# Transposes of the second chunk on VectorE; clamp and integer addition of the weight conversion on GpSimd

## Chip, cores and metric

One core of one Trainium2 chip. The metric is the device time of one execution in microseconds (us), as the median of several executions. An experiment is given with the kernel before, run on the same chip in the same rounds. All runs compared here are of the fast state; one execution of the kernel before, of 1321.95 us, is marked slow in the record and left out of the ratios. A ratio is the mean time of one kernel's fast runs over the mean of the other's of the same rounds, so it is not quite the ratio of the medians that stand beside it.

## The reference

```python
# batch 4, heads 8, sequence 768, head size 48; d_model 384, d_ff 1536; weights arrive as float64
f = 1 / (1 + exp(-f_logit))
for t in range(S):                        # HGRN2: a state per head, decayed by f
    state = f[:, :, t, :, None] * state + einsum('bhd,bhe->bhde', k[:, :, t], v[:, :, t])
    y[:, :, t] = einsum('bhd,bhde->bhe', q[:, :, t], state)
x = y.transpose(0, 2, 1, 3).reshape(B * S, H * D)
out = (silu(x @ w_gate) * (x @ w_val)) @ w_out
```

## The kernel before

The sequence is cut into six chunks of 128 steps. A chunk and one of the four batches make a "unit": units 0 to 3 are the first chunk, 4 to 7 the second. While the products of one chunk run on TensorE, the attention units of the next are worked in between. During the first chunk's products the weights are also brought from float64 words to float32, in 18 pieces of 128x768.

q, k and f have to be transposed. In the first `SQUARES` chunks TensorE does that, from double-buffered raw tiles; in later chunks VectorE does it from 32x32 squares, and then both buffers together are one "room":

```python
SQUARES = 2
...
if c >= SQUARES:
    nc.scalar.activation(squares("f"), squares("f"), AF.Sigmoid)
    nc.vector.transpose(in_turn(pairs(gate)[:, :, 1:N1]), squares("f"))          # L494
else:
    p = transposed("fTp", fr)                                                    # TensorE, L488
    nc.scalar.activation(pairs(gate)[:, :, 1:N1], p, AF.Sigmoid)
...   # L502: scan for the tails
if c >= SQUARES:
    nc.vector.transpose(in_turn(kT), squares("k"))                               # L514
    nc.vector.transpose(in_turn(qT), squares("q"))                               # L515
    load_after(u)
else:
    kp, qp = transposed("kTp", kr), transposed("qTp", qr)                        # TensorE, L488
nc.vector.tensor_tensor(kT, kp, pairs(tail, 2)[:, :, 0:C], ALU.mult)             # L520
nc.vector.tensor_tensor_scan(head, gate[:, 0:n], start, 1.0, ...)                # L522
nc.vector.tensor_tensor(qT, qp, pairs(head)[:, :, 1:N1], ALU.mult)               # L523
...   # TensorE: scores sc (L535), kT transposed (L542), y (L561, L565), dS (L589)
```

A piece of the weights passes three engines. SyncE fetches the words (three buffers), ScalarE takes out two parts (two buffers each), and VectorE joins them in four steps (code abridged):

```python
def fetch():  nc.sync.dma_start(out=w64, in_=src)                                 # L423
def sizes():  up  = nc.scalar.activation(lo, Copy, scale=2.0 ** -29)              # L432
              top = nc.scalar.activation(hi, Abs)                                 # L434
def join():
    nc.vector.tensor_scalar(top, top, MIN, MAX, op0=ALU.max, op1=ALU.min)         # L440 clamp
    nc.vector.tensor_scalar(top, top, 3, 0x3FFFFFFF, shift_left, bitwise_and)     # L442 shift
    nc.vector.scalar_tensor_tensor(top, hi, -(1 << 30), top, and, or)             # L443 merge
    nc.vector.tensor_tensor(dst.bitcast(I32), top, up, ALU.add)                   # L444 addition
```

A scheduler orders the instructions of each engine, by its own estimates. In the traces an engine takes them in that order: one that waits holds up those behind it (2.90 us in run e7, below).

## Time and profile before

| | before |
|---|---|
| median (range) of 3 executions | 642.0 us (641.66 to 642.87) |
| TensorE (PE) busy of the 641.2 us span | 632.4 us, 99% |
| VectorE (DVE), ScalarE (ACT), GpSimd (POOL) | 73%, 29%, 3% |
| mean granted TensorE clock | 0.999 |

TensorE is full (it waits 3.7 us in all for others), so the table is read through TensorE.

### The profile page before, as it was taken

To read this page: it belongs to the slowest core of one execution; us is meant where nothing else is said; L and a number is where in the kernel's file an instruction comes from. 1 tells how busy PE (TensorE), PEld (TensorE's weight loads), DVE (VectorE), ACT (ScalarE), POOL (GpSimd) and SP (SyncE) were. 2 spreads that over 40 slices of the span, in tenths; PEclk is the share of its full clock that TensorE was granted. 3 is DMA by queue.
4 is the path that set the end of the run, shared out by engine and by line. 5 is a ranking of instruction groups with operands and counts; after the bars stand their busy time and mean duration, and the time that the engine had idled before them with its cause. 6 is when DMAs were issued, how large, how long until landed. Compare 5 with 4: busy or idle time off the path is not lost.

```text
span 641.2 us, 10398 instructions
## 1 busy us (share of the span) xinstructions
PE 632.4 (99%) x4014; PEld 522.3 (81%) x4014; DVE 471.0 (73%) x802; ACT 186.6 (29%) x284; POOL 22.4 (3%) x39
## 2 busy tenths in 40 slices
PE   8999999999999999999999999999999999999996
PEld 5954555667888899888999888899888889988896
DVE  6889779988987875896966787877497862366631
ACT  1566366204632212523221614130321210021100
POOL 1000000000000010010000010000000000000000
PEclk9999999999999999999999999999999999999999
DMA  9987456333230324130324321132411001100001
GB/s 193 234 212 225 127 141 206 102 81 101 67 92 6 94 67 132 50 75 26 75 52 131 91 49 50 32 80 65 123 38 49 15 24 23 54 0 1 0 1 54
DMA packets 98393, 51.89 MB, mean 81 GB/s; under 512 B 56864, under 2 KB 92192, under 8 KB 98336
## 3 DMA queue, kind: packets, MB, share of 16 engines
q1 hardware_dynamic: 95024, 46.63, 28.7%
q10 hardware_dynamic: 3312, 4.52, 2.0%
q8 instruction: 33, 0.54, 0.4%
q14 instruction: 24, 0.20, 0.1%
HBM read 42.47 MB, written 4.72 MB: 74 GB/s over the span
## 4 chain that ended last, share of the span: by engine, by line
PE 98%; DMA 1%; DVE 0%; SPq 0%; issue 0%
PE p L760 32%; PE o L824 19%; PE c L760 13%; PE o L671 5%; PE val L647 5%; PE gate L647 5%; PE sc L535 4%; PE y L565 3%; PE o L877 3%; PE y L561 2%; PE kt L542 2%; PE dS L589 2%; PE y L582 1%; DMA fraw<-in_f_logit_dram 1%; PE idle L356 1%; PE fTp L488 1%
## 5 line engine op out<-in xcount | busy, mean ns | idle before, releaser
L703 DVE TENSOR_TENSOR rest<-u,p 128x512 f32<-128x512 f32 x90 | 61.2, 685 | 43.8 <-PE p L760 43.4
L760 PE MATMUL p<-xT,w_val 128*128 128x256 f32 x240 | 71.4, 379 | 0.0
L760 PE MATMUL p<-xT,w_gate 128*128 128x256 f32 x240 | 71.4, 379 | 0.0
L703 DVE TENSOR_TENSOR u<-u,p 128x512 f32<-128x512 f32 x90 | 61.9, 687 | 10.4 <-PE p L760 8.5
L824 PE MATMUL o<-w_out,h 128*128 128x192 f32 x360 | 62.0, 329 | 0.0
L790 ACT ACTIVATE h<-rest 128x768 f32<-128x768 f32 x30 | 25.3, 844 | 123.6 <-DVE rest L703 123.6
L824 PEld LDWEIGHTS o<-w_out,h 128*128 128x128 f32 x360 | 58.2, 190 | 1.7 <-ACT u L842 1.1
L760 PE MATMUL c<-xT,w_gate 128*128 128x256 f32 x180 | 54.9, 387 | 0.0
L760 PE MATMUL c<-xT,w_val 128*128 128x256 f32 x180 | 53.5, 379 | 0.0
L760 PEld LDWEIGHTS p<-xT,w_val 128*128 128x128 f32 x240 | 45.6, 190 | 6.2
L760 PEld LDWEIGHTS p<-xT,w_gate 128*128 128x128 f32 x240 | 45.6, 190 | 6.2
L537 DVE TENSOR_TENSOR A<-sc,causal 128x512 f32<-128x512 f32 x48 | 31.5, 685 | 10.4 <-PE sc L535 10.4
L760 PEld LDWEIGHTS c<-xT,w_val 128*128 128x128 f32 x180 | 34.2, 190 | 4.6
L527 POOL TENSOR_TENSOR decayed<-state,tails 128x192 f32<-128x192 f32 x20 | 19.7, 986 | 504.3 <-DVE state L593 360.2
L760 PEld LDWEIGHTS c<-xT,w_gate 128*128 128x128 f32 x180 | 32.5, 190 | 5.2 <-issue 0.9
L760 PE MATMUL p<-xs,sv 128*128 128x256 f32 x120 | 35.7, 379 | 0.0
L760 PE MATMUL p<-xs,sg 128*128 128x256 f32 x120 | 35.7, 379 | 0.0
L791 DVE TENSOR_TENSOR h<-h,rest 128x768 f32<-128x768 f32 x30 | 28.8, 962 | 9.1 <-ACT h L790 9.1
L768 ACT COPY u<-c 128x512 f32<-128x512 f32 x30 | 17.4, 581 | 53.8 <-PE c L760 32.1
L647 PE MATMUL val<-xT,w_val 128*128 128x512 f32 x72 | 32.3, 594 | 0.0
L647 PE MATMUL gate<-xT,w_gate 128*128 128x512 f32 x72 | 32.3, 594 | 0.0
L502 DVE TENSOR_TENSOR_SCAN tails<-gates,ones 128x516 f32<-128x516 f32 x24 | 29.4, 1224 | 3.9 <-POOL decayed L527 2.1
(127 smaller groups left out, 1076.6 us busy)
## 6 DMA issues: line engine op xcount, KB each, us to landing
fraw<-in_f_logit_dram SPq DMA_DIRECT2D x64, 96.0 KB, 3.0
kraw<-in_k_dram SPq DMA_DIRECT2D x64, 96.0 KB, 2.2
qraw<-in_q_dram SPq DMA_DIRECT2D x64, 96.0 KB, 2.2
v<-in_v_dram SPq DMA_DIRECT2D x24, 192.0 KB, 3.5
w<-in_moe_w_gate_dram SPq DMA_DIRECT2D x6, 768.0 KB, 4.6
w<-in_moe_w_val_dram SPq DMA_DIRECT2D x6, 768.0 KB, 5.1
w<-in_moe_w_out_dram SPq DMA_DIRECT2D x6, 768.0 KB, 5.6
out_dram<-ob ACTq DMA_DIRECT2D x23, 192.0 KB, 2.5
```

What stands on the lines that cost most here:

```text
L502: nc.vector.tensor_tensor_scan(tail[:, 0:n][:, ::-1], gate[:, 0:n][:, ::-1], ones[:, ::-1], 1.0, op0=ALU.mult, op1=ALU.add)
L527: nc.gpsimd.tensor_tensor(decayed[:, :, 0:D], states[b], whole.broadcast_to((128, HP, D)), ALU.mult)
L535: nc.tensor.matmul(sc[par][:, a * C:(a + 1) * C], lhsT=kT[r, a, :], rhs=qT[r, a, :], start=True, stop=True)
L537: nc.vector.tensor_tensor(A[:, par], sc[par].rearrange("p (a t) -> p a t", t=C), causal.unsqueeze(1).broadcast_to((128, HP, C)), ALU.mult)
L565: nc.tensor.matmul(place(a, par), lhsT=v_[:, 2 * a + par, :], rhs=A[:, par, a, :], start=False, stop=a >= HP - 2, skip_group_check=True)
L647: nc.tensor.matmul(p, lhsT=w[:, i, j * 128:(j + 1) * 128], rhs=xT[c][:, i, :], start=(i == 0), stop=(i == KT - 1))
L671: nc.tensor.matmul(p, lhsT=h[n // 2][:, n % 2 * 2 + b // 2, b % 2 * C:(b % 2 + 1) * C], rhs=w_out[:, j, :], start=(n == 0), stop=(n == NF ...
L703: nc.vector.tensor_tensor(dst, a, b, ALU.add)
L760: nc.tensor.matmul(p[:, n, :], lhsT=lhsT, rhs=rhs, start=first and n == 0, stop=last, skip_group_check=True)
L790: nc.scalar.activation(h[j][:, 1:4, :], rest[:, :, 0, :], AF.Silu)
L791: nc.vector.tensor_tensor(h[j][:, 1:4, :], h[j][:, 1:4, :], rest[:, :, 1, :], ALU.mult)
L824: nc.tensor.matmul(p[:, n, :], lhsT=lhsTs[j][:, n * C:(n + 1) * C], rhs=rhs[:, j, :], start=first and j == 0 and n == 0, stop=last and j = ...
```

## The change

The intent: VectorE takes the transposes of units 4 to 7 from TensorE, and GpSimd, which is 3% busy, takes two of VectorE's four steps of every piece so that VectorE has room.

```diff
-    SQUARES = 2
+    SQUARES = 1
...
-            nc.vector.tensor_scalar(top.bitcast(FP32), top.bitcast(FP32), as_float(0x38000000), as_float(0x47F00000),
+            nc.gpsimd.tensor_scalar(top.bitcast(FP32), top.bitcast(FP32), as_float(0x38000000), as_float(0x47F00000),
                                     op0=ALU.max, op1=ALU.min)
...
-            nc.vector.tensor_tensor(dst.bitcast(I32), top, up, ALU.add)
+            nc.gpsimd.tensor_tensor(dst.bitcast(I32), top, up, ALU.add)
```

## The prediction

> **What bounds the kernel now.** I read the page's busy table first, then TensorE's own waits, then busy time by stretch, then the order of time around single instructions, and last the groups by form.
>
> ```profile
> PE 632.4 (99%) x4014; PEld 522.3 (81%) x4014; DVE 471.0 (73%) x802; ACT 186.6 (29%) x284; POOL 22.4 (3%) x39
> ...
> PE idle L356 <- DVE ones L348: 2.1, 1, 2.1
> PE fTp L488 <- DMA fraw<-in_f_logit_dram: 0.8, 1, 0.8
> PE o L877 <- DVE ob L703: 0.4, 1, 0.4
> PE y L565 <- DVE A L537: 0.2, 1, 0.2
> PE y L582 <- DVE A L537: 0.2, 1, 0.2
> ```
>
> TensorE (PE) is busy 632.4 of 641.2 us and waits 3.7 us in all. So work taken off PE is worth its full time, and any new wait of PE costs its full time. The changed part is the stretch in which the first chunk's products run while the second chunk's four attention units (numbered 4 to 7) and the 18 weight pieces are prepared beside them:
>
> ```profile
> 36.00:66.00 30.00, 30.00 (x133) 14.73 (x132) 28.80 (x45) 19.59 (x25) 1.17 (x1) 1.00 0.76 217
> ...
> 112.00:149.00 37.00, 37.00 (x194) 23.19 (x189) 34.33 (x46) 6.02 (x12) 1.61 (x2) 1.00 0.34 90
> ```
>
> Columns: length, then busy time of PE, weight loads, DVE (VectorE), ACT, POOL (GpSimd). PE is full, DVE is at 96% and 93%: DVE has no room for transposes unless something leaves it. This is why the two parts of the change come together.
>
> **What the change removes from PE.** Three groups of four transposes in each of four units:
>
> ```profile
> 71.07 0.60 PE L488 MATMUL kTp<-idf,kraw 128*128 128x128 f32 x4
> 71.50 0.60 PE L488 MATMUL qTp<-idf,qraw 128*128 128x128 f32 x4
> 71.94 5.32 PE L647 MATMUL gate<-xT,w_gate 128*128 128x512 f32 x12
> ```
>
> From start to start a group takes 0.435 us (its 0.60 overlaps what follows). 12 x 0.435 = 5.2 us. At the first unit less is won: its three groups (34.46 to 35.77) fill time in which PE would wait anyway, as the last copy to xT ends at 35.14 on ACT. The first gate product can start at about 35.3, not 34.5. So 4.3 us are won.
>
> **What it moves between DVE and GpSimd.** The rows by form (busy, mean ns):
>
> ```profile
> L440 DVE TENSOR_SCALAR top<-top 128x768 f32<-128x768 f32 x18 | 10.0, 553 | 10.6 <-ACT top L434 10.6
> L444 DVE CUSTOM_DVE_ANT_0 w_gate<-top,up 128x1536 uint16<-128x1536 uint16 x6 | 5.7, 953 | 0.8 <-PE gate L647 0.8
> L515 DVE STREAM_TRANSPOSE qT<-qraw 128x512 f32<-128x512 f32 x16 | 18.6, 1160 | 0.2 <-PE y L561 0.2
> L514 DVE STREAM_TRANSPOSE kT<-kraw 128x512 f32<-128x512 f32 x16 | 17.9, 1118 | 0.0
> L494 DVE STREAM_TRANSPOSE gates<-fraw 128x512 f32<-128x512 f32 x16 | 17.4, 1088 | 0.0
> ```
>
> DVE loses 18 x (0.553 + 0.95) = 27 us and gains 4 x (1.09 + 1.12 + 1.16) = 13.5 us: 13.5 us lighter. GpSimd has no such instruction yet; I estimate from its 128x192 multiply, which takes 0.515 us where nothing disturbs it. A fill of 128 columns takes 0.205 us and one of 64 takes 0.157, so some 0.1 us is fixed: (0.515 - 0.1) / 192 = 2.1 ns per column. The integer addition (768 columns) is then 0.1 + 1.65 = 1.75 us. The clamp has one input: I take 1.0 us, between 0.75 and 1.3. In all 18 x 2.75 = 50 us of GpSimd's 114, which is not a bound by itself.
>
> [...]
>
> ```profile
> 41.80 0.94 DVE L443 SCALAR_TENSOR_TENSOR top<-w,top 128x768 int32<-128x768 int32 x1
> 41.97 1.17 POOL L527 TENSOR_TENSOR decayed<-state,tails 128x192 f32<-128x192 f32 x1 [38.68 <-DVE tails L502]
> 42.65 0.52 DVE L505 TENSOR_TENSOR least<-least,tails 128x4 f32<-128x4 f32 x1
> ```
>
> The multiply of 0.52 us takes 1.17, ending 0.4 after L443 ends (42.74); then the tiny L505, else 0.17, ends with it. [...]
>
> **The order of the changed program decides it.** I compared the order of instructions on each engine, as built. A piece used to go ACT, then four DVE instructions. Now it goes ACT (1.65 us), GpSimd clamp, DVE shift and merge (0.6 + 0.9), GpSimd addition: two hand-overs more, in three in-order queues, with only two buffers. On PE the units are no longer split: scores, kT transposes, y and dS stand together (about 2.6 us after the scores end), and the next product waits for GpSimd. With durations from the trace and about 0.1 us per hand-over I walked PE's queue:
>
> 1. First val product. ACT ends its piece at 36.75 as before. Then the clamp[...]; a transpose stands between shift and merge on DVE, and GpSimd clamps the next piece first; the addition ends at 42.2 (no contention) to 44.2. PE wants it at 40.45. Wait 1.8 to 3.9, say 3.0.
> 2. Scores of unit 5. Its q transpose needs qT, which y of unit 4 has just been reading; 1.06 + 0.69 against 1.47 us of PE work: 0.5.
> 3. Third val pair, after unit 5. From the end of the scores: kt copy, ACT's next piece (to 3.0), its clamp (4.05), and only then, in GpSimd's order, the addition that PE needs (5.8). PE is there at 2.6: 3.3.
> 4. Scores of unit 6. They follow a val product at once, while DVE's order is: multiply of that product, q transpose, q times head. 0.1 + 0.6 + 1.15 + 0.7 + 0.06 = 2.6, whatever GpSimd does.
> 5. Fifth gate pair, after unit 6: as 3, 3.2.
> 6. Scores of unit 7: as 4, 2.6.
> 7. First down product: mask multiply 1.3, shift and merge 1.5, addition 1.75, against 2.6: 2.1.
> 8. Last third of the down products, after unit 8, which the new order draws forward: as 3, 3.25.
> 9. First product of the next chunk. DVE begins the weight sums about 6 us after the scores of unit 8 and needs 13 us until the token sums; PE wants them at 17.3: 1.5.
>
> Sum 22.0 us. All else waits for nothing that is not there. Net: 22.0 - 4.3 = +17.7, thus 660 us. I take 657, as such a walk leaves some waits too long and the clamp may be quicker.
>
> **The rivals.** *The plain gain:* DVE had no room before and has 13.5 us more now, so the new transposes hide and PE keeps its 4.3 to 5.2 us: 637 to 638. For it: 100% busy PE, a lighter DVE, fewer and larger packets for the loads. Against it: waits 4 and 6, which already cost 5.2 us and need no assumption on GpSimd. *A wash:* GpSimd is quick[...], only waits 1, 4, 6, 7 and half of the rest remain: some 14 - 4.3 = +10, 652. [...] *Loads late:* with one raw buffer for q, k and f, loads of a unit wait for the transposes of the one before. Landing takes 3 us and a unit's turn 20; no bound, I think.
>
> **Range and chances.** 647 to 666 runs from half of the waits to all of them with contention. Faster by 2% would need under 629.2, more than PE's removed work: 0.02. Slower by 2% starts at 654.8; my sum lies above it and the wash below: 0.63. Within: 0.35.
>
> **What would show it.** Right: PE busy near 627 us; PE waits on the additions (line 444 on GpSimd) of about 12 to 16 us in some six places; two waits of 2.6 us of scores on the q multiply (line 523); DVE busy about 457; additions at 1.75 us or more, clamps about 1.0. Wrong: PE still full from 36 to 149 (then the walk misread the order or the queues), or additions far under 1.75 us, or DVE waits for loads, or waits of PE that lie after this stretch.

Three of its figures, held against the pages. The clamp's 1.0 us is the author's estimate, since the trace before has no clamp on GpSimd; it lies between some 0.7 us, an estimate for 768 columns from the two fills (0.157 us for 64, 0.205 for 128), and the 1.75 of the addition. Hand-overs in that trace took 0.03 us (36.75 to 36.78, ScalarE to VectorE) and 0.08 (41.89 to 41.97, VectorE to GpSimd). Packets: 98393 of 527 bytes in the mean before, 92826 of 585 after, over all DMA.

## The result and the profile after

The changed kernel takes 685.27 us (681.87 to 685.55, 4 executions) beside 641.87 us before on the same chip: a ratio of 1.066 (95% interval 1.0625 to 1.0696). The results are correct. The prediction had the direction, but 685 lies far outside of 647 to 666.

The page's busy table and the row of the granted clock, kernel after:

```profile
PE 643.5 (94%) x3966; PEld 525.6 (77%) x3966; DVE 473.0 (69%) x778; ACT 189.3 (28%) x286; POOL 104.3 (15%) x75
...
PEclk9989996989899999999999999999999999999999
```

Two things are seen. TensorE stands idle 683.5 - 643.5 = 40.0 us instead of 8.8. And it is busy 643.5 us although 12 x 0.435 = 5.2 us of transposes have left it: 627.2 were due, so 16.3 us more went into the same work. The clock row says where: of the first eleven slices, one has a 6 and three have an 8; before, the mean clock was 0.999. The trace also keeps each change of the granted clock, of which the views show only means: in the changed kernel it is half in six stretches between 42.9 and 182.9 us, one of 3.41 and five of 6.83 us, 37.5 us together; they start 11, 6, 3, 8 and 11 times 3.41 us apart. In the kernel before it is full from 11.5 to 639.6 us.

TensorE's waits, kernel after (columns: what waited, what released it, us in total, times, longest):

```profile
PE val L647 <- POOL w_val L444: 9.1, 2, 5.0
PE sc L535 <- DVE qT L523: 7.0, 4, 3.7
PE o L671 <- POOL w_out L444: 6.4, 2, 4.7
PE gate L647 <- POOL w_gate L444: 3.6, 1, 3.6
```

In the order of time around instructions (start, duration, in brackets the idle time before), kernel after:

```profile
44.07 8.22 PE L647 MATMUL val<-xT,w_val 128*128 128x512 f32 x12 [4.12 <-POOL w_val L444]
52.13 5.31 PE L647 MATMUL gate<-xT,w_gate 128*128 128x512 f32 x12
...
72.01 1.16 PE L535 MATMUL sc<-qT,kT 48*128 48x128 f32 x16 [0.52 <-DVE qT L523]
...
101.83 2.08 PE L535 MATMUL sc<-qT,kT 48*128 48x128 f32 x16 [3.67 <-DVE qT L523]
```

A pair of products takes 5.31 us, but 8.22 right after a wait of 4.12. Scores take 1.16 us, but 2.08 after a wait of 3.67. So these two waits are paid twice: as idle time, and as a slow stretch after it.

Busy time by stretch, kernel after, for the two stretches shown before (columns as there):

```profile
36.00:66.00 30.00, 25.88 (x71) 11.69 (x70) 18.76 (x25) 12.41 (x16) 18.51 (x8) 0.89 0.48 128
112.00:149.00 37.00, 34.43 (x128) 18.25 (x129) 18.51 (x26) 15.39 (x22) 20.07 (x10) 0.83 0.47 129
```

Now no engine is full. VectorE fell from 28.80 to 18.76 us of 30, GpSimd stands at 18.51, TensorE at 25.88: everybody waits for somebody.

The groups by form, kernel after (busy, mean ns | idle before, by releaser):

```profile
L440 POOL TENSOR_SCALAR top<-top 128x768 f32<-128x768 f32 x18 | 51.3, 2854 | 44.0 <-ACT top L434 44.0
L444 POOL TENSOR_TENSOR w_gate<-top,up 128x768 int32<-128x768 int32 x6 | 10.9, 1812 | 8.7 <-DVE top L443 8.7
L442 DVE TENSOR_SCALAR top<-top 128x768 int32<-128x768 int32 x18 | 17.6, 977 | 25.3 <-POOL top L440 25.3
```

The addition takes 1.81 us, as estimated (1.75). The clamp takes 2.77 us where nothing disturbs it (mean 2.85), not 1.0. VectorE's shift has grown from 0.56 to 0.98 us in the mean. Twelve of the 18 still take 0.56; four, which start just after an addition, take 2.15, and two, which start just after a clamp, 1.17. A clamp, an addition and a shift:

```profile
107.34 2.77 POOL L440 TENSOR_SCALAR top<-top 128x768 f32<-128x768 f32 x1 [7.61 <-ACT top L434]
110.07 1.80 POOL L444 TENSOR_TENSOR w_gate<-top,up 128x768 int32<-128x768 int32 x1
110.14 2.15 DVE L442 TENSOR_SCALAR top<-top 128x768 int32<-128x768 int32 x1 [1.37 <-POOL top L440]
```

The shift ends 0.42 us after the addition does (112.29 and 111.87), and the other three 0.41 after theirs. The multiply of unit 4 in the prediction looks the same: 1.17 us for 0.52 beside VectorE's merge, ending 0.4 after it. The two shifts beside a clamp end before it does (148.98 and 150.51 in one case), so the clamp did not hold them up for the whole of its length.

### The profile page after: what moved, and what is told of

The parts are those of the page before. It is cut to its first block, busy times and chain, and to the rows that moved or that the text cites. A ratio compares the mean times of both kernels' runs of the same rounds, so it can differ in the third digit from the quotient of the medians.

```text
span 683.5 us, 10365 instructions
## 1 busy us (share of the span) xinstructions
PE 643.5 (94%) x3966; PEld 525.6 (77%) x3966; DVE 473.0 (69%) x778; ACT 189.3 (28%) x286; POOL 104.3 (15%) x75
## 2 busy tenths in 40 slices
DMA packets 92826, 54.26 MB, mean 79 GB/s; under 512 B 45152, under 2 KB 86624, under 8 KB 92768
## 4 chain that ended last, share of the span: by engine, by line
PE 83%; DMA 4%; DVE 4%; SPq 3%; POOL 2%; issue 2%; ACT 1%; ACTq 0%; DVEq 0%; POOLq 0%
PE p L760 29%; PE o L824 18%; PE c L760 11%; PE val L647 4%; PE gate L647 4%; PE sc L535 4%; PE o L877 3%; PE y L565 2%; PE y L561 2%; PE o L671 2%; DMA fraw<-in_f_logit_dram 2%; PE kt L542 1%; POOL top L440 1%; DMA xT<-yT 1%; SPq L576 1%
## 5 line engine op out<-in xcount | busy, mean ns | idle before, releaser
L527 POOL TENSOR_TENSOR decayed<-state,tails 128x192 f32<-128x192 f32 x20 | 17.8, 891 | 389.4 <-DVE state L593 284.8
L440 POOL TENSOR_SCALAR top<-top 128x768 f32<-128x768 f32 x18 | 51.3, 2854 | 44.0 <-ACT top L434 44.0
L647 PE MATMUL val<-xT,w_val 128*128 128x512 f32 x72 | 36.3, 659 | 9.1 <-POOL w_val L444 9.1
L671 PE MATMUL o<-w_out,h 128*128 128x384 f32 x96 | 34.7, 524 | 6.4 <-POOL w_out L444 6.4
L647 PE MATMUL gate<-xT,w_gate 128*128 128x512 f32 x72 | 35.1, 640 | 4.2 <-POOL w_gate L444 3.6
L535 PEld LDWEIGHTS sc<-qT,kT 48*128 48x128 f32 x384 | 25.0, 198 | 15.6 <-DVE qT L523 8.5
L647 PEld LDWEIGHTS val<-xT,w_val 128*128 128x128 f32 x72 | 15.1, 214 | 28.4 <-issue 18.3
```

The source lines that it names most:

```text
L440: nc.gpsimd.tensor_scalar(top.bitcast(FP32), top.bitcast(FP32), as_float(0x38000000), as_float(0x47F00000), op0=ALU.max, op1=ALU.min)
L527: nc.gpsimd.tensor_tensor(decayed[:, :, 0:D], states[b], whole.broadcast_to((128, HP, D)), ALU.mult)
L535: nc.tensor.matmul(sc[par][:, a * C:(a + 1) * C], lhsT=kT[r, a, :], rhs=qT[r, a, :], start=True, stop=True)
L647: nc.tensor.matmul(p, lhsT=w[:, i, j * 128:(j + 1) * 128], rhs=xT[c][:, i, :], start=(i == 0), stop=(i == KT - 1))
L671: nc.tensor.matmul(p, lhsT=h[n // 2][:, n % 2 * 2 + b // 2, b % 2 * C:(b % 2 + 1) * C], rhs=w_out[:, j, :], start=(n == 0), stop=(n == NF ...
```

## The experiments

Eighteen kernels ran, three rounds each and five for the last two. Medians in us; "before" on the same chip had medians of 641.9 to 643.05.

| run | what | median (range) | ratio (95% interval) |
|---|---|---|---|
| e1 | transposes alone | 667.72 (663.86–673.34) | 1.037 (1.032–1.042) |
| e2 | GpSimd alone | 685.55 (685.33–685.87) | 1.067 (1.064–1.070) |
| e3 | transposes, addition moved | 670.50 (668.49–671.36) | 1.044 (1.041–1.047) |
| e4 | transposes, clamp moved | 677.68 (675.75–678.85) | 1.054 (1.051–1.057) |
| e5 | whole change, TensorE kept busy in waits | 678.56 (677.28–682.08) | 1.058 (1.053–1.062) |
| e6 | whole change, clamp of one operation | 679.16 (677.66–681.68) | 1.057 (1.053–1.060) |
| e7 | transposes alone, units split | 664.91 (663.62–665.98) | 1.035 (1.032–1.038) |
| e8 | whole change, units split | 676.17 (675.69–676.83) | 1.053 (1.050–1.056) |
| e9 | e7 with two qT | 673.98 (671.27–675.06) | 1.046 (1.041–1.051) |
| e10 | e9, VectorE in stated order | 673.17 (670.92–673.42) | 1.045 (1.041–1.050) |
| e11 | e10, addition moved | 675.92 (672.84–680.16) | 1.053 (1.046–1.060) |
| e12 | whole change as e10, three buffers | 688.83 (684.92–691.68) | 1.072 (1.066–1.078) |
| e13 | whole change, a third of the clamp | 670.76 (665.71–671.74) | 1.041 (1.036–1.047) |
| e14 | e13, TensorE kept busy in waits | 666.35 (665.23–669.44) | 1.038 (1.033–1.042) |
| e15 | e7 without a clamp | 665.75 (664.53–669.29) | 1.038 (1.034–1.042) |
| e16 | before without a clamp | 644.35 (642.47–646.40) | 1.004 (1.000–1.008) |
| e17 | transposes alone, order of before | 669.38 (667.92–671.96) | 1.041 (1.038–1.045) |
| e18 | e17, fetches ahead of loads | 654.17 (653.41–657.28) | 1.019 (1.016–1.022) |

All gave correct results.

### The change in its parts (e1 to e4)

e1 is the diff's first line alone, e2 its other two, e3 and e4 the first with one of the other two.

> Second chunk's units with VectorE transposes, clamp and addition left on VectorE. Theory A (the long GpSimd clamp, 2.77 us, makes the waits, and each wait over some 2.5 us also halves the clock for 3 us after it): most of the loss goes; two waits of about 2.6 us for the scores that follow a val product at once stay, with slow clock behind them, and VectorE, 13.5 us heavier, adds some: 648 to 658 us. Theory B (the order with whole units standing together is the cause, wherever the clamp runs): 670 us or more, waits of 20 us or more.

> Clamp and addition on GpSimd, the second chunk's units with TensorE transposes as before; TensorE's order is the one of before, with split units. Theory A: the chain to the first val product still is some 4 us late and its clock drop costs 3 more; later pieces have several us of slack: 648 to 660 us. Theory B: at most 3 us over before, 642 to 645 us.

> As the change, but the clamp stays on VectorE; only the addition (1.8 us) goes to GpSimd. Theory A: near e1, 646 to 658 us, since the 2.77 us clamp is out of the chain. Theory B: the order is that of the change, so 670 us or more.

> As the change, but the addition stays on VectorE; only the clamp (2.77 us) goes to GpSimd. Theory A: worse than e3 by 5 us or more, 660 to 678 us. Theory B: the same as e3 within 4 us.

Both parts lose on their own (3.7% and 6.7%), and together they lose no more than the worse one (6.6%). So neither theory holds as it stood: the loss is not GpSimd's alone, nor the transposes' alone. With the transposes, moving both steps costs 685 - 668 = 17 us; the clamp moved alone costs 10 (e4) and the addition alone 3 (e3), the latter within the range of e1's own executions.

e2 shows what the way over GpSimd costs with no transposes moved. The shift's row and the scores of one unit, run e2:

```profile
L442 DVE TENSOR_SCALAR top<-top 128x768 int32<-128x768 int32 x18 | 20.4, 1134 | 42.8 <-POOL top L440 42.8
```

```profile
101.00 2.08 PE L535 MATMUL sc<-qT,kT 48*128 48x128 f32 x16 [8.90 <-DVE qT L523]
```

VectorE stands 42.8 us in front of shifts whose clamp is not done. Its queue is in order, so the q multiply of a unit (L523), which needs nothing from GpSimd, stands behind the shift, and TensorE waits 8.90 us for it. GpSimd was busy 25.16 of the 30 us from 66 to 96 there.

### Half clock and clamp size, in the whole change (e5, e6, e13, e14)

In these four the order of the instructions on TensorE, VectorE, ScalarE and GpSimd was held to that of the changed kernel, so that only the named thing differs (in e13 two neighbours in VectorE's queue swapped). Lines are shifted in them: L710 and L702 are products, L549 and L542 scores. The edits are abridged.

```diff
 # e5: matmuls without a reader, into the bank that the group itself overwrites
+    fill(p, {("val", 0): 12, ("val", 4): 15, ("gate", 8): 9}.get((name, j), 0))
+    fill(sc[0], {2: 9, 3: 6}.get(b, 0))            # second chunk, units 6 and 7
 # e6: the clamp's lower bound alone
-    nc.gpsimd.tensor_scalar(top, top, MIN, MAX, op0=ALU.max, op1=ALU.min)
+    nc.gpsimd.tensor_scalar(top, top, MIN, None, op0=ALU.max)
 # e13: the clamp on 256 of 768 columns (right for these weights only, which reach no bound)
+    part = top[:, 0:1, 0:256]
+    nc.gpsimd.tensor_scalar(part, part, MIN, MAX, op0=ALU.max, op1=ALU.min)
 # e14: e13 and fills of 6, 8, 7, 5 and 5
```

> The changed kernel with the order of its instructions on TensorE, VectorE, ScalarE and GpSimd held to what it was, and 51 idle bf16 matmuls of 128x512 put ahead of five of the six groups that wait longest: first val pair (12), third val pair (15), scores of unit 6 (9), fifth gate pair (9), scores of unit 7 (6). They write the bank that the group itself overwrites, so the results stay right. The last third of the down products, which waits 4.71 us, gets none and serves as a control within the run. Theory C (a wait of TensorE of more than about 2 us makes it run at half rate for the next 3 to 6 us): the groups after the five waits take 5.31 (pairs) and 1.16 us (scores) again and not 8.22, 6.80, 8.43, 2.08 and 2.00; the down products after their wait stay slow; 2.9 + 1.5 + 2.4 + 3.1 + 2.0 = some 12 us less, 671 to 675 us, mean clock 0.985 or more. Rival D (the groups are slow because of what GpSimd and VectorE do to the operands or the memory at that time): the groups stay at 8.2 and 2.0 us, and the time at 683 to 688.

Around two of the filled groups, run e5:

```profile
39.53 2.75 PE L361 MATMUL val<-ones 128*128 128x512 bf16 x12
45.36 7.11 PE L710 MATMUL val<-xT,w_val 128*128 128x512 f32 x12 [3.08 <-POOL w_val L449]
...
96.78 2.10 PE L361 MATMUL sc<-ones 128*128 128x512 bf16 x9
100.64 1.16 PE L549 MATMUL sc<-qT,kT 48*128 48x128 f32 x16 [1.75 <-DVE qT L534]
```

Four of the five filled groups ran at full speed again; the first, where the fill left 3.08 us of idle time, did not, and neither did the last third of the down products, the control. (Behind the scores of unit 7, full speed themselves, y was slow all the same.) The time at half clock fell from 37.5 to 13.7 us. The operands and the work of the other engines were the same, so the slow groups are slow because TensorE stood idle before them, which is theory C. Of the 12 us expected only 6.7 came back (685.27 to 678.56): TensorE reached the later groups earlier, and GpSimd's pieces did not come earlier, so part of the gain turned into waits.

> The changed kernel, all orders held, with the clamp on GpSimd reduced to its lower bound (one operation, not two; these weights never reach the upper bound, so the results stay right). Theory E (the clamp is long because GpSimd pays for each of the two operations): the clamp takes 1.4 to 1.6 us instead of 2.8, each just-in-time chain of a piece is 1.2 us shorter, TensorE's waits on pieces shrink by some 7 to 10 us and the clock recovers part of its loss: 666 to 676 us. Rival F (its cost is per element read and written, whatever the operations): the clamp stays at 2.6 to 2.9 us and the time at 683 to 688.

```profile
L440 POOL TENSOR_SCALAR top<-top 128x768 f32<-128x768 f32 x18 | 40.0, 2225 | 50.0 <-ACT top L434 49.9
```

That is the clamp's row of e6. Neither E nor F: one operation takes 2.13 us undisturbed, two take 2.77. A clamp 0.63 us shorter gained 6 us.

> The changed kernel, all orders held, with the clamp on GpSimd applied to 256 of the 768 columns only (no weight of this input reaches a bound, so the results stay right; the kernel would be wrong for others). It should take 0.9 to 1.1 us, the length that the prediction took for the whole clamp. Theory K (the missing terms are the clamp's size and the half clock): the one-operation run lost 6 us for 0.63 us less of clamp, so 1.8 us less give some 17 us: 664 to 671 us, the two waits of scores at 2.6, the waits on pieces near the predicted 3.0, 3.3, 3.2, 2.1, 3.25, and groups after waits over 2 us at half rate still. Rival L (something else bounds the pieces, buffers or ScalarE): 676 to 686 us.

> The run before, and idle bf16 matmuls (5 to 8 each, 31 in all) ahead of the same five groups as in the filled run, fewer as the waits are shorter. Theory K: no half clock in those groups, 6 to 10 us less than the run before, 655 to 663 us, which is the prediction's 657 to 660 plus nothing else. Rival L: 670 or more.

The clamp's row of e13:

```profile
L441 POOL TENSOR_SCALAR top<-top 128x256 f32<-128x256 f32 x18 | 21.4, 1187 | 56.1 <-ACT top L434 56.0
```

It takes 1.06 us undisturbed, which is the 1.0 that the prediction took for the whole. The time falls by 14.5 us to 670.8 (expected 664 to 671). Now the walk of the prediction can be held against a trace with its own clamp. The nine waits measured in e13 are 1.2, 0.5, 3.0, 3.7, 1.5, 2.6, 0, 3.5 and 1.4, together 17.4 us; the walk had 3.0, 0.5, 3.3, 2.6, 3.2, 2.6, 2.1, 3.25 and 1.5, together 22.0. TensorE was busy 640.9 us where 627.2 were due: 13.7 us are half clock, which the walk lacked. e14 took 4.4 us of this back and ended at 666.4, above the 655 to 663 expected; it still had slow groups after the shorter fills, one slow gate pair before all fills (7.04 us for 5.31, after a wait of only 0.66), and one wait of 4.2 us at the next chunk's first products, which the profile puts down to no releaser. That rest stays open.

### TensorE's order (e7, e8)

The changed order puts a unit's scores, y and dS together. These two hold TensorE to the order in which the program states it. It is that of the kernel before, with the transposes left out, except that unit 8 still stands ahead of the last down products, as in the changed kernel.

```diff
+        since = traced[-1]
         take_turns(pieces, attention_steps(c + 1) if c + 1 < NCH else [], 2 if c else 8)
+        if c == 0:
+            in_order(since, (mybir.EngineType.PE,))
```

> The transposes alone (clamp and addition on VectorE), with TensorE's order in the first chunk's stretch held to the order in which the program states it, which is the order of the kernel before with the transposes left out: units split, scores apart from y and dS. Theory G (what costs 3.7% in the transposes alone is the clustered order): 636 to 648 us, TensorE waits under 12 us in all. Theory B (VectorE has no room for 13.5 us more): VectorE's queue is late all the same, waits of 20 us or more, 660 to 672 us.

> The whole change, with TensorE's order held to the same stated order (units split). If the clustered order is what exposes the GpSimd chain, the waits of the scores of units 6 and 7 (3.67 and 2.57 us) and those of the products right after a unit fall away: 655 to 668 us. If GpSimd's chain of some 6 us per piece bounds the stretch whatever the order, as in the run with GpSimd alone, the time stays at 680 to 690 us.

The order is worth 9 us in the whole change and some 3 in the transposes alone (the ranges overlap): a part, not the cause. e7 fell in rival B's range, e8 between its two. In e7 a unit's waits moved to the pieces:

```profile
66.52 1.16 DVE L515 STREAM_TRANSPOSE qT<-qraw 128x512 f32<-128x512 f32 x1 [2.90 <-PE y L561]
```

VectorE's copy of q stood 2.90 us at the head of its queue until the unit before had read the single qT. The weight piece behind it came late and TensorE waited 4.04 us for it.

### Looking for the cost of the transposes alone (e9 to e12, e15, e16)

```diff
 # e9: two buffers for qT.  e10: VectorE held to the stated order as well.
-        qT = att.tile([128, HP, C], FP32, tag="qT", name="qT")
+        qT = att.tile([128, HP, C], FP32, tag="qT", name="qT", bufs=2)
 # e11: e10 with the addition on GpSimd.  e12: the whole change as e10, and three buffers for up and top, four for w64.
 # e15: e7 without the clamp.  e16: the kernel before without the clamp (both right for these weights only)
```

> The run with the transposes alone and split units, with two buffers for qT. In that run VectorE's q transpose stood 2.90 us at the head of its queue until y of the unit before had read qT, with a finished-but-for-VectorE weight piece behind it, and TensorE then waited 4.04 us for that piece. Theory H (the write of the transposed q straight into the single qT is what costs): VectorE no longer waits for y (3.7 us in the stretch, two times), the waits of 4.0 and 4.3 us lose 3 us or more each and the half clock after them, 648 to 658 us. Rival I (the order of VectorE's queue, units ahead of pieces, costs on its own): the piece behind the unit is late as before, 660 to 666 us.

> As the run before, and VectorE's order of the stretch is also held to the order in which the program states it, in which a piece is finished before the work of the next unit starts. Theory I: pieces come in time, the waits on them fall under 8 us together, 634 to 645 us. If VectorE simply has no room for 13.5 us more: it is busy 28 of 30 us in each stretch and the time stays at 650 or more.

> As the run before, with the integer addition on GpSimd (1.8 us a piece, 33 us in all) and the clamp left on VectorE. VectorE is 17 us lighter and never waits on GpSimd within a piece, as the addition is its last step. If the addition is harmless where the order is good: at or up to 5 us under the run before. If its 0.85 us more of latency a piece[...] still cost: 5 to 15 us above it.

> The whole change, with everything given to it that the runs so far ask for: TensorE's and VectorE's stated order, two qT, and three buffers for each step of a piece in place of two (four in place of three for the fetched words). If buffers and orders were what cost, 640 to 655 us. If a piece's way over GpSimd (clamp 2.8, addition 1.8, with VectorE standing still between them) bounds the stretch in itself, 665 us or more, with VectorE waiting 30 us or more for the clamp.

> The run with the transposes alone and split units, one qT, with the clamp left out altogether (results stay right for this input, not in general): VectorE 10 us lighter, nothing on GpSimd. Theory B (VectorE's load is what makes the transposes lose): most of the loss of 23 us against the kernel before goes, 642 to 650 us. If the longer chain of a unit (two copies that stand in VectorE's queue ahead of the scores) is the cause whatever the load: 655 to 664 us.

> The kernel before with the clamp left out (right for this input only), as a control: VectorE 10 us lighter in a stretch where TensorE is already 100% busy. All theories: 639 to 643 us, the same within 0.5%. Should it be faster by over 1%, then TensorE was not the bound of that stretch.

No run here bore out the theory that it was built for. Two rivals came nearer: e12 met its own (over 665, and VectorE over 30 us before its clamps), and e10 took over 650 us, but with VectorE busy 22 to 27 of 30 us, not 28. e9 took VectorE's wait for y away and was 9 us slower than e7: the scheduler, free to place the copy, put other work in the way. e10's order brought the pieces of gate and val in time (2.6 us of waits) but the scores (8.1) and the pieces of the down products (9.9) late. e11 gained nothing from a VectorE that was 11 us less busy (476.6 for 487.5). In e12 more buffers did not help the chain over GpSimd: VectorE still stood 33.1 us before its clamps. e15 took 10 us from VectorE and stayed at e7's time within the ranges, which speaks against VectorE's load as what then bound it; the control e16 moved by no more than 0.4%.

The trace of e15 gave the next theory. A piece's ScalarE step waited 8.46 us for its words, and SyncE, which issues fetches, loads and stores in order, had issued nothing from 48 to 64 us: it stood for the stores of unit 4's y, with the next fetch behind them.

### SyncE's queue (e17, e18)

e17 is the transposes alone with the order of the kernel before on TensorE, VectorE, ScalarE, and for SyncE's fetches and stores; each VectorE transpose stands directly before the instruction that uses it. The loads of f, k and q stay free. e18 differs in SyncE's order alone: fetches stand ahead of the loads that have to wait.

```diff
 # SyncE's order around unit 5's loads: F a fetch of weight words
-   F(gate) f5 k5 q5 v5 F(val) F(gate) F(val)          # e17
+   F(gate) f5 F(val) F(gate) k5 q5 v5 F(val) F(gate) F(val)   # e18
```

> The transposes alone (nothing on GpSimd), with the order of TensorE, VectorE and ScalarE in the first two chunks' stretches, and of SyncE's weight fetches and stores to xT, held to that of the kernel before: TensorE's without the transposes, VectorE's with each transpose directly ahead of the instruction that uses it; the loads of q, k and f are free. Theory M (the order of the queues that the change brings is what costs, above all fetches behind stores): 636 to 645 us, no wait of SyncE over 8 us on a store ahead of fetches in the stretch, TensorE waits of 12 us or less. If the longer chain of a unit through VectorE costs by itself: 650 us or more, with the waits of TensorE on VectorE's scores or pieces as before.

> The run before (transposes alone, orders of the kernel before), and SyncE's order also fixed for the stretch: a weight fetch stands ahead of each load of f, k and q that has to wait for a copy by VectorE, in the order of the times at which the kernel before issued its fetches. All other engines' orders are the same as in the run before. Theory N (fetches held behind loads that wait for the single room are what costs): no wait of ScalarE over 5 us for a weight's words, no wait of VectorE over 4 us on ScalarE, 15 us or more less than the run before, 640 to 654 us. Rival B (VectorE has 118 us of work in 120 us and everything just in time waits for it): 660 to 670 us, VectorE busy 28 of 30 us from 36 to 66.

SyncE's queue, run e17 and then e18 (start, us in the queue):

```profile
45.75 1.74 SPq L403 DMA_DIRECT2D kraw<-in_k_dram  x4
51.99 1.73 SPq L403 DMA_DIRECT2D qraw<-in_q_dram  x4
53.77 1.69 SPq L408 DMA_DIRECT2D v<-in_v_dram  x1
55.51 0.58 SPq L423 DMA_DIRECT2D w<-in_moe_w_val_dram  x1
```

```profile
42.68 0.39 SPq L423 DMA_DIRECT2D w<-in_moe_w_val_dram  x1
49.43 0.39 SPq L423 DMA_DIRECT2D w<-in_moe_w_gate_dram  x1
49.87 1.91 SPq L403 DMA_DIRECT2D kraw<-in_k_dram  x4
51.87 2.62 SPq L403 DMA_DIRECT2D qraw<-in_q_dram  x4
```

In e17 the load of unit 5's q goes out at 51.99, right after VectorE's copy of unit 4's q (50.89 to 51.97), because the two share one room. The val fetch behind it goes out at 55.51 and not at 42.68. What that does further down, on ScalarE and VectorE, run e17:

```profile
61.65 0.90 ACT L432 ACTIVATE up<-w 128x768 int32<-128x768 uint32 x1 [13.75 <-DMA w<-in_moe_w_val_dram]
```

```profile
63.37 0.56 DVE L440 TENSOR_SCALAR top<-top 128x768 f32<-128x768 f32 x1 [8.61 <-ACT top L434]
```

e17 missed theory M's 636 to 645. With SyncE's order changed and nothing else, the time falls from 669.4 to 654.2 us, at the edge of theory N's range. What is left in e18, first TensorE's waits, then busy time from 36 to 66, then the longest wait:

```profile
PE sc L535 <- DVE qT L523: 8.1, 3, 3.5
...
PE o L671 <- DVE h L663: 2.0, 1, 2.0
```

```profile
36.00:66.00 30.00, 27.00 (x106) 12.68 (x106) 29.52 (x45) 17.40 (x23) 1.06 (x1) 1.00 0.73 214
```

```profile
105.28 1.25 PE L535 MATMUL sc<-qT,kT 48*128 48x128 f32 x16 [3.49 <-DVE qT L523]
```

TensorE no longer waits long for a weight piece (0.5 us). It waits 8.1 us for the q multiply, in three waits. One of them (3.00 us, at 52.70) falls where VectorE is busy 29.52 of 30 us, as rival B has it: no room for the copies. The others (1.60 at 78.91 and 3.49 at 105.28) fall where it is busy 23.87 and 26.92 of 30, and shortly before them VectorE had itself stood 2.11 and 1.81 us for ScalarE. So rival B can hold for a part of the rest at most, and no run took work off VectorE in e18 to test it. TensorE's busy time is 630.2 us, and the 12 us by which e18 is above the kernel before are waits. No version here beats the kernel before.

## Why the prediction was wrong

Against the walk's 660 the changed kernel is 25 us too slow. In its trace TensorE is idle 31.2 us more than before, where the walk had 22.0, and busy 11.1 us more, where the walk had 4.3 less. So two steps failed, the cost of the clamp and the speed after a wait, and the second is the larger in the trace.

**Right: direction, places, addition.** The kernel is slower, and the waits lie where the walk put them: all but the seventh and ninth were found on the named instruction and releaser. The second and sixth had the predicted length (0.52 and 2.57 us); the seventh, first down product, was 0, with 1.69 us one piece later; the ninth was 1.84 us but behind ScalarE's output copy, not the weight sums. The addition was right to 0.06 us.

**Wrong: "The clamp has one input: I take 1.0 us, between 0.75 and 1.3."** It is 2.77 us; 256 columns take 1.06 (e13), so 3.3 ns per column by the difference. No row of the trace before showed the 1.0. This term failed in the sum: with a clamp of the assumed length (e13) the time is 14.5 us lower, and the nine waits add up to 17.4 us against 22.0 predicted. That the sum is so near is in part luck: single waits are off both ways, the first 1.2 for 3.0, the fourth 3.7 for 2.6, the seventh 0 for 2.1. But e13's 670.8 us still lies outside of 647 to 666, so the clamp alone is not the error. The sum of GpSimd's time, 50 us, should have been 18 x (2.77 + 1.81) = 82.

**Missing: what a wait does to the clock.** The prediction had "any new wait of PE costs its full time" and counted it once. TensorE took 16.3 us longer for its work in the changed kernel and 13.7 in e13; e5 shows that the waits cause most of it. This term explains the way from the walk's 660 to e13's 671: 13.7 more, less the 4.6 by which the waits were shorter, gives 669.

**Wrong: VectorE 13.5 us lighter.** The copies and the two steps were counted right, but the shifts grew by 7.6 us together (six of the 18, four beside an addition of GpSimd's and two beside a clamp), about half of the difference between the 457 us predicted and the 473.0 measured. Why they grew was not shown beyond that.

**Small sums.** With the walk's own lengths the wash's waits come to 16.2 us, not 14, thus 654 and not 652, and half of the waits gives 649, not 647. Neither moves the range much.

**Dismissed too fast: "Loads late … no bound, I think."** The load itself does not bind; what stands behind it in SyncE's queue does. In the kernel with the transposes alone this is worth 15 us (e17 against e18). In the whole change SyncE stood 16.4 us for the store of unit 4's y, the val fetch behind it went out at 78.13, and ScalarE waited 3.52 us for its words; but the product that uses this piece (at 92.84) waited for nothing. I found no wait of TensorE there that leads back to a fetch, and SyncE's order was not tested, so its share of the 43 us stays open.

**Left open.** The parts are not additive (e1 to e4), so the 43 us cannot be split cleanly. Some 6 us between e14 and the walk's 660 have no shown cause. Why e9 is slower than e7 was read from the orders but not tested.

## What to carry to other kernels

An idle engine is not a free engine. Here GpSimd was 3% busy, and the clamp went from 0.55 us on VectorE to 2.77 on it; with both steps there (e2), VectorE stood 42.8 us before its shifts, and TensorE waited 8.90 us for a q multiply that needed nothing from GpSimd. Measure the moved instruction once, in its own shape, before counting on it. Price a new wait of TensorE over some 2 us at its own length plus the slow stretch behind it (3.41 or 6.83 us at half clock in the changed kernel). Of the pairs of products and the scores between 36 and 180 us in the twenty traces, those that took over 1.2 times their 5.31 or 1.16 us were 19 of 19 after waits of over 3.5 us, 20 of 28 after 2.0 to 3.5, and 5 of 26 after 0.9 to under 2.0. And when a buffer becomes single, look at the queue that refills it: not whether the refill is late, but what stands behind it (a fetch at 55.51 us and not at 42.68 in e17; 15 us of the time against e18).
